# Attention scores as four 64x64 tiles instead of one zero-padded 128x128 matmul, in a fused Linformer and MLP-mixer kernel

## The chip, the cores and the metric

The kernel runs on one core of one Trainium2 chip. The metric is the device time of one execution in microseconds (us): 417.4, 418.6 and 418.67 us in three runs of the kernel before, median 418.6 us. What this measurement can tell from no change is about 0.3%, or 1.3 us.

## What is computed

A Linformer attention on `q`, `k`, `v` of shape (8, 8, 1024, 64), batch, heads, tokens, head width, feeds an MLP mixer; all inputs and the output are float32, the kernel works in bfloat16 with float32 sums.

```python
k_proj = einsum('ks,bhsd->bhkd', E, k)      # 1024 tokens to 64
v_proj = einsum('ks,bhsd->bhkd', F, v)
scores = q @ k_proj.T / 8                   # (1024 x 64) @ (64 x 64) a head
attn   = softmax(scores)                    # over the 64 projected tokens
x      = attn @ v_proj                      # heads side by side: (8, 1024, 512)
u      = x + (relu(x.T @ w_tok1) @ w_tok2).T        # 1024 -> 256 -> 1024 over tokens
out    = u + relu(u @ w_ch1) @ w_ch2                # 512 -> 1536 -> 512 over channels
```

## The kernel before

**The work of a batch.** Eight batches go through a front and a back. The front is: projection of keys and values (`kv_proj`), turning of keys and queries (`k_transpose` and `q_transpose_pe` on TensorE for batches 0 and 1, `k_transpose_dma` and `turn_q` by DMA transposes later), `scores`, `attend`, and the token mixing (`token1...`, `token2...`). Its result `u` is turned, by TensorE for batch 0 and by a DMA transpose (`turn_u`, tile uT) for the others. The back is the channel mixing in two blocks of 512 tokens a batch: `up_set` (line 1193), three sets a block, and `down_block` (line 1301). Up, down and, from batch 2 on, the token products take seven products where the plain scheme takes eight; VectorE makes the sums that this needs.

**Two tokens on the partitions.** Token 8p + si of a batch lies on partition p. A turned query tile qT of a head has the 64 widths of an even si on partitions 0 to 63 and those of the odd si on 64 to 127, and 512 columns. So that one matmul serves both, the turned keys kT hold the same 64x64 block twice on the diagonal of a 128x128 tile, with zeros in the other two blocks (a memset in line 307 puts them there once). `scores` (line 634) is one 128x128 matmul of 512 columns for a head; ScalarE takes the exponential of its bank into the tile a (line 643). The values vb of a head are laid out the same way, twice on the diagonal, each with a column of ones that gives the sum of the softmax; `attend` multiplies 128 columns of a with them (lines 657 and 693, 130 columns), and VectorE divides (reciprocal in lines 669 and 705, multiply in 674 and 710).

**Projection.** `kv_proj` (line 529) uses TensorE in two halves of 64 columns: the keys' product goes to output partitions 0 to 63 and the values' to 64 to 127, alternately, from 128-row operands. From batch 2 on, ScalarE copies the keys twice into kb (which also has zero blocks, line 308) and the values twice into vb, 64x512 each, and a DMA transpose makes kT from kb, 128 x 1024.

**What sets the order.** Nothing is scheduled at run time. A planner holds one list of jobs; the string ORDER gives the order of all of them, SPOTS the PSUM bank of each tile, FILLS the places in that order where a matmul on zeros is put in (`blank`, line 440), so that TensorE does not go idle in the opening. Each engine gets its instructions in that order and works them off in that order; semaphores hold an instruction back until what it needs is there. Loads go through POOL's queue, with eight in flight; the DMA transposes through SP's. ORDER, SPOTS and FILLS come from a search outside of the kernel.

**The opening.** E and F, then q, k and v of batch 0 in pairs of heads, the token weights (wt1, wt2), the channel weights (wc1, wc2) and batch 1 are loaded one behind the other; LOADS and ORDER say in which order. Batch 0 is worked pair by pair as it arrives.

Of the kernel before, what the change touches and what calls it, by code (L numbers as in the profile page):

```python
# [15 lines left out]
    "0P0Q0R0S000T0201030U0W0X040V0s0+1G0-050u0t1I1H0x1J0y0z1L1O101209241N0v1K1P0w131M26111A1B1Q1D0625071S"  # L16
    "1T172A1g18080A1C0B1E0C1a1415191b2C1R1k2B1h1i1o1c1F1l1j1d1n1m161X1p1Y1q2D1s1U1r2E1Z1t0D1u1e1f1x1V1W1v"
    "0E272H2F0G0H1w29281+2V2I211y1-2a0F1z222b20232G2P2W2Q2M2c2J2f2X2S2g2N2K2Y2Z2d2L2R2h2e2T2O2k2i2l2U2t0I"
    "2m2p2n332u2j2x2q2r2o342-2y0J0K2v3B2s300Y2z35313C0Z2w2+320c3T3P0a3R3l3Q3F3U3D3V3J3K360d370e3W3X3Z3m38"
    "0L0N413G3p3Y3a3q3n3b3o0b3S0g0O3c420M0h3r3L3s3E3d390f3M0i3f433e3A3t3g3H0j3u3I4547465044513v48493w5x4g"  # L20
    "4h523x5y5z4k4i4A4j3y534B4J604D4l3N4o4E5-544K5+4m0o614C4F3h4p554r4L3z4n4s0p574R4q0k584u5A4S0q3-4H0l4t"
    "3j0m62634v563O654O646N666P4w594P6O5C404T6Q3+4x6e6W4Q6f6X6g3i674U6T6B6Y6Z696L5I684I3k6U6V4V6R6J6K6a6A"
    "5J6S6b6F6G5D4G6c6d0r5K5M6C4MAH6D6E6j4y4W6H5BAI6r6I0n5N6s6k6l4N4Y6u6t6m6n6h6i6o6v4Z5L5P705O6p4X6w714c"
    "726x5Q6q736z5R4a5a6y6+6-75745S5E7677787B5bAJ7C797H5T7A5c7I4d5U7D7K7E5i7J7LAK6M7NA97M7Q7FAB7G7O7R7S7P"
    "AL4b7T5V5G4z5F4+AAAOAC5W5Y5X7V5j4eAN7UAM7XAQ7W4-5f7Z7YAP7a7c7g5g7e7d7h5h7f5d7i5lAV5kAh5mAW7jAZAb5e5H"
    "Ai7bAX5n5ZAcAaAe7l7pAfAYAd5p7qAmAj817r7sAg7nAnAkAlAuAT7tAxAo5qAvAw7o7u7m82ApAr7wAy85Az5r5o7vAqAsAtA+"
    "B583B0A-5t7x86BB887y847-BC7z7k89B1B6ASB2B7BDAUARB3B880BE8J87B9BF7+8BBAB4BJ8ABM8KBGBK8LBLBHBI8M8NBP8D"
    "BNBS8OBQBO5uBR8Q8b8P8CBTBVBU8EBXBW8RBYBZ8T8y8S8cBaBb8UBc90Bd8+Be918V94Bf5v8zBgAD8WBj92Bh95Bk9E97Bi9F"
    "93Bn968FBo8-Bl9GBr9I98Bs9A9J9HAFBmBp8HBq8I99AEEn8dBuBw8X9CEp9B9L9M8jBxBvBt9WBy9OErEoEq8Z9PAG9X8g8k8h"
    "BzB+5sEj8YEk4f9DB-9aC48iC19Y8mC08lC29bC59dC79Z9c8G9e8nC68e9K8aC89f8oCB8f9g9NEs9iC99QCC8pCDEl8q8uCA9j"  # L30
    "CG9hCH8r8sC3CJE-8vEzCEF09R9oEx8wCFCLE+CNEyCO9p9kCbEv5wF1F4CK9qCP9wEmF5CQF29SF39mCMCR9xCcCIF69U9TCSCf"
    "F7CUCVCgF8Cd9y9tFBCXFCCT8t9uF9FDCYCWEw9VFGCeCtFH9vFACu9lCZCiCaFOCjDWFPCvCw9zChFECxFIDXCyFFFL9+ClCkCz"
    "FJFMDYFN9-FQ9nFRC+FSCmFKCnCoC-A1FTD0FUFVD9DaA2D1DbFWEuDAD3CpA3FXFYDeFZFaEtDfDZDcDdFd9rD4D5CqDh9sIrDB"
    "DiFeA0FbFfItFcCrA5DkFh8xInFgIsIvD2FiCsIoFjA6DoFnIuFoFkA7D7FlFmDHFrD8DpDlDgFpFvDIFsDjFqFtDmDsA4DnFwDt"
    "DJFyDEFxF+D6DFFzDqG0F-DvDGDCG8G1DrDwFuDKG2G3DyG9G5G4DLG6GBE4DMDuGCDzE5DDDxE8DNIpIqIwE9GAGDGFD+GGGEGH"
    "EBDOECE6GIDPGKD-G7J3EAGJGLEDDSJ4E7I-DQIzJ0J1EEEGGRJ2EFJ5J8GSGNDTGPGMEMJ9J6J7JDEHDUDRE0JAJBJEE1EIENGT"
    "GfEOE2GgGVJCEKA8EUGjGWEVJFGOGkJGERJHEWGQELGhESJNGmGiGUETJOGYGXJIGnI+JKDVGZGpGxJLIxGbEXEJGqJMJPHaGyJJ"
    "GaHcEYMrJSJTGcJQGzGdJRJUE3EZHeG-EbGlJVGeIyJWHbG+H0EPJXH2GoGrHdJYJZGsHfHgHiJaJbHjH3JcEQJdEcEaHhJfHsJh"
    "EdJgJiH5MsHlGtJeEfHmJjHoEgH1H6HtJkJmEhHpJlJnH4EiHkGuJoHnJrHDJsGvJpJqH7JvHqH8JtJwH9HAHBJzJxJuJ+HrMvK0"
    "HwK2HxMxK1JyHEK3K4HzJ-K5MtK6HFHuHIKCK9MyHLK7H+MwHvKDMzI0I1HMKFHyKAHCK8EeHNKGI8HGI9GwHJICHKKJIAKHKEHO"  # L40
    "IBIDKKKIKMHPKLH-HQM+KNHHIFKON7IGI2KBHSN8IEKPN3IIHTNCHRKRN4MuKVIJIHI3HUKTIKN5KWNDIQKZN9ILN1M-KaN6KXHW"
    "IRNAKYNBISIMNEKjNHHXNIKUI4NFNGI6IYHYNJKkIZNKNLNRKcKdI7NOKnIOKoKlKfIVNSNPNQNMIWKmIaKQNNKSHVKgKbI5NTIX"
    "NUKeINLeKqK-L0IbNVKhN2IcNYL3KiITNZNWKrNaL4NbIPL6NXIdNcL7IUNdKpIeIfNeKsNfIgL1KtIjKvNgNlN0NhIhNjKwL2L5"
    "L8IkLHL9LBNmKxNiNkKuKzLfNnIlLCQwNoLiLINqNpNrNsLALDIiKyQzLjLkLgLJK+LELFNtNuNvLlNwLmHZNxLwLGLMLxQ-NzNy"
    "N+O1O2LnN-LNLOL+R1LyO4LpLPO6O5O0O8LhR0O9L-LzQ+LQLoM1LSO7LqO3LRLrLTQvImOBOGOALuODOCOELvQyLsMCM2OHQxOJ"
    "M4LtOKM0LKONLLM3M5OIMDR2LUMGOLOOMHM6OPLWMEMJMFOQOSOMM7LVOFLXMKOTMIOVMLOXORLYOZLaR7MOMMRBLbMPMQMUM8R9"
    "R8MNRCOaRDLcREOWMVRARFOdOnMWOoMSMAObMcMBR4RIOrMZRJOeOcOsOpRKOuRNROOYOqR5RPMdLZOvOgOxRGOyRVRHOUMaP3Oh"
    "RWM9MeRLOfOjRSMbR6OiRTMTMfRMOkP4RaRbOlRUMRMgOmP7RQOtRXRRMhRYP5RZMjMXPiOwRcMYPmP6RdReOzMiRfPjO+PkMkMn"
    "P8RgPLR3RhMlPnPARiPlMoRjPBP9PqPoRkUzPpPDMpRlRnPCO-PMRoRpV1PFRmRqPEPrMmMqPtRrV3PNRsRtPuPsPGPHLdP0V5Ru"
    "RvPTPwRzP1V2PIV4RwPJRxRyP+P2R+PUPxPvS1PVS5R-S2PQS0S3S6U+P-PyPzQGS8SAQ0SKQ2QHQ1S9SBQIPKS4Q3QJSCPRS7SL"  # L50
    "SDQ4Q5SFQKSNPSSESHQ6QLSGQ8PWSPPXQNQ7SISOPYSRV0V6U-QASSSMQBQ9QOSTSQPOQCPaSUPPSWSXQMVBPbSVQQVCV7QRV9QY"
    "SJQDSdQPPZPcV8SZVAQZVDVEVFSbQSQTSeSfPeVIShSYSgPfQaSiQgVJVGVKQUSkQWPgQEVNScQhSrVOVPVHPdQdVLVVQeSsSlSv"
    "VWVSSwVMSaQiQfSnStSjSoVQTnVTTmVUSyVXT7VRSuSzToQjSmSxVaVYQXVZQVVcVdVeS-S+QFSpSqVbQkVfQbT0TqT8T1QlQcQn"
    "TBT2T9VgVhQmViTrTCTsVjTEQoTpVkVlQpTAVnQrVpTFTHQsTDTtVqVmTIU2QtVoTuTGT3VrVsVtTwVuTvTJU3TxVvVzVwT5TKU6"
    "TyVxVyU4T+V-TzTPV+U7T6W0U0TLT-U5W1W5U9W6UKT4TNW2UAW3ULU1W7WATQW8QqUCTRW4TMW9TOUOUDUPTUWCU8UMTVWDPhQu"
    "WBTXWEWKWFWHTWUBWGTYTaWITZUNURUETbUSUFTSUQWLWNTcWPTTUTTeWOTdUWWRTiUXWJUUWdTfWZWaWSWMUVTjWeWrWfTgWbWT"
    "WUWgWQUcWsWhWiWcUdWvWkUGTkWVUYUeWtWuWlUkX7UaUIUHUlUhWjWWUmWnUiThUJWXUjX8WwWmXBWyX9UZWoWzUnXAWYWpWqUo"
    "UbW-XCX0UpUfWxW+XEXDXFXGUgUrXHXJXqUqUsXmX1XoXKY6XnUvUtXIX2XPXrY7XuX3UuYAUwXsX5XLX4XNUxX6XpXvXQY8YBYD"
    "XwXxXtXRYEXXXUXyY9XzYGYOXYY0XVTlYHY1XWXMYPYSYQYCXaY2YTYFYRYVXZXbYWY3XcXOYUYXYIXSXeYaXfYJYKYbYgY4XTYM"
    "YYXgYZYcXdYhYeX+YLYiXiYNX-UyXhYlXjYmYdYfYoXkYxYnYjYkYsYpYqYrXlYuYvY5Z5YtYyYwZ7YzY-Y+Z0Z1Z6Z2Z8Z3Z9Z4"  # L60
    "ZA"
)
SPOTS = (
    "3142613427007634307612314207426673103142670116377263077463615421302542313140341042376756766765577757"
    "5677567656575676776765677012402414535120342241300556757665577667657656757670616706243123414252534103"
    "1030217767656565656566664736746140534132101500435323042776765656566656666572764742531530452410441031"
    "0201575666656765656667373675631354342042453105031532566576565656665666657476371031410300534153443125"
    "327676656565666566662726706421140051545432102101214756"
)
FILLS = (9, 9, 14, 14, 14, 14, 14, 14, 16, 16, 16, 16, 16, 16, 27, 27, 27, 42, 42, 72, 81, 81, 84)  # L70
# [118 lines left out]
def kernel(  # L189
# [86 lines left out]
    vb = tile_of([P, H, 2, D1], BF16, "vb")  # L276
    kT = tile_of([P, H, 2, KP], BF16, "kT")
# [4 lines left out]
    kb = tile_of([P, H, 2, D], BF16, "kb")  # L282
# [9 lines left out]
    a_t = [tile_of([P, 2, S2], BF16, f"a{i}") for i in range(2)]  # L292
# [4 lines left out]
    rdn_t = [tile_of([P, 2, 4], F32, f"rdn{i}") for i in range(2)]  # L297
# [9 lines left out]
    nc.vector.memset(kT, 0.0)  # L307
    nc.vector.memset(kb, 0.0)
# [198 lines left out]
    def kv_proj(b, h0, hn, due, block=False, apart=False):  # L507
# [3 lines left out]
        t = 8 * max(cols, 128) / 2400 + 0.22  # L511
        if block:
            k_to = [kb[i * KP : (i + 1) * KP, hs, i, :] for i in range(2)]
        else:
            k_to = [kp[:, hs, i, :] for i in range(2)]
        v_to = [vb[i * KP : (i + 1) * KP, hs, i, 0:D] for i in range(2)]
        of = {"k": (0, k_to, "kb" if block else "kp", ET_sb, k_sb), "v": (KP, v_to, "vb", FT_sb, v_sb)}

        def side(names):
            bk = Bank(stream[0], full=False)  # L520
# [5 lines left out]
            def mm():  # L526
                for si in range(NSI):
                    for n in names:
                        nc.tensor.matmul(  # L529
                            view(n), of[n][3][:, si, :], of[n][4][:, hs, si, :],  # L530
                            start=(si == 0), stop=(si == NSI - 1),
                        )

            pl.add(
                "PE", t, t, mm, reads=[("EFT", 0), ("EFT", 1)] + [(n, h) for n in names for h in heads],
                takes=[bk], prio=due,
                after=[("vb", i, h) for i in range(2) for h in heads] if "v" in names else (),
            ).mms = NSI * len(names)
            unit = scalar() if block else next(sides)
            for n in names:  # L540
# [67 lines left out]
    def q_transpose_pe(hp, due):  # L608
# [19 lines left out]
        )  # L628

    def scores(h, due):  # L630
        bk = Bank(stream[0], full=False)
        pe(
            1, 512,
            lambda: nc.tensor.matmul(  # L634
# [938 lines left out]
```

## Time and profile before

| | |
|---|---|
| median of three runs | 418.6 us (417.4 to 418.67) |
| span of the profiled execution, first to last instruction | 415.5 us |
| granted TensorE clock, mean | 1.000 |
| busy: PE, DVE, ACT, POOL | 409.8, 358.8, 227.4, 66.7 us |
| matmuls | 3845 |
| scores, line 634 | 64 matmuls of 512 columns, 379 ns each |
| projections, line 529 | 192 matmuls of 64 array columns |
| DMA transposes: uT, qT, kT | 14, 12 and 6; 4.3, 5.2 and 3.2 us from issue to landing |
| DMA | 62.47 MB, mean 150 GB/s; 201 to 207 GB/s from 10 to 80 us |

The profile gives the profiled execution no other time than its span; the median of the runs is 3.1 us above it, which is what lies around the span. The duration of one matmul in the table is from its start to its modelled end, and matmuls overlap: what one costs the engine is the distance from its start to the next start, which the timeline shows. So a busy share of PE near 100% does not say by itself that TensorE is at its limit; the distances do.

### The profile page before, as it was taken

Reading aid. Unit: us, or ns where it says so; the run is one execution under the profiler, and the core shown is the slowest. Engines: PE = TensorE matmul, PEld = TensorE weight load, DVE = VectorE, ACT = ScalarE, POOL = GpSimd, SP = SyncE. Lnnn points to the kernel's source line nnn. Section 1 sums busy time; section 2 is a strip of 40 time slices with the busy share of each in tenths; the row PEclk is TensorE's granted clock in tenths of the full one; section 3 lists DMA queues with packets and bytes.
Section 4 is the critical chain, followed back from the end, with each engine's and each line's share of the span. In section 5 each row is a group of like instructions: output and inputs, shape, how many; then the busy total and the mean of one; then the engine's idle time right before and its main releaser. Section 6 shows DMA issues by size and latency. Waiting matters only on the chain.

```text
span 415.5 us, 9448 instructions
## 1 busy us (share of the span) xinstructions
PE 409.8 (99%) x3845; PEld 349.0 (84%) x3845; DVE 358.8 (86%) x774; ACT 227.4 (55%) x434; POOL 66.7 (16%) x105
## 2 busy tenths in 40 slices
PE   8999999999999999999999999999999999999996
PEld 4589888688898889888898888988898889998885
DVE  2489898899899988989988997888999998897696
ACT  1758875376745655564465537365573656254620
POOL 8444111013010400130101220102200010000100
PEclk9999999999999999999999999999999999999999
DMA  8999999996999898679979899488982403212314
GB/s 162 204 202 205 206 206 224 168 138 101 232 167 209 137 233 134 104 170 221 217 106 189 113 184 198 83 165 135 231 152 53 100 11 144 50 53 52 153 50 154
DMA packets 96827, 62.47 MB, mean 150 GB/s; under 512 B 62096, under 2 KB 92304, under 8 KB 96784
## 3 DMA queue, kind: packets, MB, share of 16 engines
q0 software_dynamic: 35088, 45.09, 55.4%
q1 hardware_dynamic: 61056, 16.00, 22.8%
q10 hardware_dynamic: 640, 0.79, 0.5%
q8 instruction: 30, 0.49, 0.5%
q14 instruction: 13, 0.11, 0.1%
HBM read 59.24 MB, written 16.78 MB: 183 GB/s over the span
## 4 chain that ended last, share of the span: by engine, by line
PE 94%; DMA 2%; POOL 2%; DVE 1%; issue 0%; POOLq 0%; DVEq 0%
PE psum L1193 35%; PE psum L1301 35%; PE psum L1004 4%; PE psum L888 4%; PE psum L529 3%; PE psum L634 3%; DMA v_sb<-in_v_dram 2%; PE psum L693 2%; PE psum L657 1%; PE psum L1105 1%; PE psum L748 1%; PE psum L1073 1%; PE psum L724 1%; DVE x_sb L674 1%; POOL k_sb L362 1%; PE psum L618 0%
## 5 line engine op out<-in xcount | busy, mean ns | idle before, releaser
L1301 PEld LDWEIGHTS <-G 128*128 128x128 bf16 x1344 | 130.2, 98 | 17.2 <-issue 0.2
L1301 PE MATMUL psum<-wc_sb,G 128*128 128x256 bf16 x768 | 104.0, 273 | 0.0
L1193 PEld LDWEIGHTS <-wc_sb 128*128 128x128 bf16 x768 | 73.9, 98 | 10.1 <-issue 0.6
L1215 ACT ACTIVATE G<-psum 128x512 bf16<-128x512 f32 x96 | 57.3, 601 | 40.7 <-PE psum L1193 40.2
L1301 PE MATMUL psum<-wT,G 128*128 128x256 bf16 x576 | 77.8, 273 | 0.0
L1229 DVE TENSOR_TENSOR G<-G 128x512 bf16<-128x512 bf16 (+1 forms) x140 | 69.1, 514 | 0.5
L1193 PEld LDWEIGHTS <-wT 128*128 128x128 bf16 x576 | 55.6, 98 | 7.5 <-issue 0.4
L1193 PE MATMUL psum<-uT,wc_sb 128*128 128x256 bf16 x384 | 56.8, 273 | 0.0
L1193 PE MATMUL psum<-S,wT 128*128 128x256 bf16 x384 | 56.8, 273 | 0.0
L1193 PE MATMUL psum<-S,wc_sb 128*128 128x256 bf16 x384 | 56.5, 273 | 0.0
L643 ACT ACTIVATE a<-psum 128x512 bf16<-128x512 f32 x64 | 37.4, 600 | 26.3 <-PE psum L634 25.9
L1341 DVE TENSOR_TENSOR o<-psum,u 128x512 f32<-128x512 f32 x59 | 40.3, 684 | 4.7 <-PE psum L1301 3.2
L1335 POOL DMA_DIRECT2D out_dram<-o x30 | 16.3, 546 | 159.4 <-DVE o L1341 124.6
L1221 ACT COPY ub<-psum 128x512 f32<-128x512 f32 x48 | 28.1, 589 | 21.9 <-PE psum L1193 18.1
L1174 DVE CUSTOM_DVE_ANT_0 G<-psum,ub 128x512 bf16<-128x512 f32 x48 | 32.8, 683 | 6.9 <-PE psum L1193 6.5
L1236 ACT COPY psum<-psum 128x512 f32<-128x512 f32 x48 | 27.7, 577 | 19.3 <-PE psum L1193 7.7
L1174 DVE CUSTOM_DVE_ANT_0 G<-psum,ua 128x512 bf16<-128x512 f32 x48 | 32.8, 684 | 5.8 <-PE psum L1193 3.0
L1221 ACT COPY ua<-psum 128x512 f32<-128x512 f32 x48 | 28.1, 591 | 17.2 <-PE psum L1193 17.0
L362 POOL DMA_DIRECT2D v_sb<-in_v_dram x18 | 13.4, 745 | 132.7 <-DMA uT<-u 76.7
L1193 PE MATMUL psum<-uT,wT 128*128 128x256 bf16 x192 | 28.7, 273 | 0.0
L710 DVE TENSOR_TENSOR x_sb<-psum,rdn 128x512 bf16<-128x512 f32 x40 | 27.5, 688 | 0.9
L634 PE MATMUL psum<-qT,kT 128*128 128x512 bf16 x64 | 22.8, 379 | 0.1
(109 smaller groups left out, 548.2 us busy)
## 6 DMA issues: line engine op xcount, KB each, us to landing
out_dram<-o POOLq DMA_DIRECT2D x30, 512.0 KB, 4.8
k_sb<-in_k_dram POOLq DMA_DIRECT2D x14, 512.0 KB, 9.3
v_sb<-in_v_dram POOLq DMA_DIRECT2D x14, 512.0 KB, 6.5
q_sb<-in_q_dram POOLq DMA_DIRECT2D x14, 512.0 KB, 12.3
wc_sb<-in_moe_w_ch_dram POOLq DMA_DIRECT2D x6, 256.0 KB, 11.6
wc_sb<-in_moe_w_ch_dram POOLq DMA_DIRECT2D x4, 384.0 KB, 15.1
k_sb<-in_k_dram POOLq DMA_DIRECT2D x4, 256.0 KB, 7.4
q_sb<-in_q_dram POOLq DMA_DIRECT2D x4, 256.0 KB, 8.9
```

The costliest lines, as they stand in the source:

```text
L362: return lambda: nc.gpsimd.dma_start(out=dst, in_=src)
L634: lambda: nc.tensor.matmul(bank(bk), kT[:, h].rearrange("p c k -> p (c k)"), qT[:, h].rearrange("p j s -> p (j s)"), start=True, stop=True,),
L643: lambda: nc.scalar.activation(out=a_t[h // 2 % 2][:, h % 2], in_=bank(bk), func=ACT.Exp, scale=scale),
L710: lambda: nc.vector.tensor_tensor(out=x_sb[:, :, h * D : (h + 1) * D].rearrange("p (n c) d -> p n c d", n=2), in0=view()[:, :, :, 0:D], in ...
L1174: nc.vector._custom_dve(TENSOR_ADD_SAT, out=out, in0=in0, in1=in1, s0=FMAX, s1=0.0)
L1193: nc.tensor.matmul(t[:, c, :], w1_of(n, dd, 2 * m + c), a_of(j, n, dd), start=(n in (1, 7) and c == 0 and dd == 0), stop=(c == 1 and dd == 1),
L1215: lambda: nc.scalar.activation(out=G[:, n, cs], in_=view(src), func=ACT.Relu),
L1221: 512, lambda: nc.scalar.copy(out=dst, in_=view("y")), writes=[(name, s % 2)],
L1229: 512 * len(both), lambda: f(out=G[:, n, c], in0=G[:, a, c], in1=G[:, b, c]), ps=False,
L1236: 512, lambda: nc.scalar.copy(out=view("y"), in_=view("x")), takes=[bk["y"]],
L1301: nc.tensor.matmul(to, G[:, G_OF[n], cc, t * P : (t + 1) * P], w2_of(n, cc), start=(n in opens and (t == 0 or alone) and cc == 0), stop=(c ...
L1341: 512, lambda: nc.vector.tensor_add(out=dst, in0=view(src), in1=u_of(sh, dh)),
```

## The change

1. **Scores in quarters.** `scores` takes pairs of heads. For a pair, four matmuls of a 64x64 tile and 512 columns each replace two of 128x128. Each uses one half of the array's rows (even or odd si) and one half of its columns (first or second head of the pair), in the order (0,0), (1,1), (0,1), (1,0). Each row half has a bank of its own; a bank holds both heads on its partitions. Batch 0 does this for one pair at a time (four blocks of four matmuls); the other batches for two pairs at a time (two blocks of eight, 14 blocks in all), which takes four banks at once. The exponentials stay 64 of 128x512, into four tiles a instead of two.
2. **Keys without zero blocks.** kT and kb have half the size, and their two memsets are gone. The keys are still copied twice (kb: 64x512 each, now with a broadcast), the DMA transpose of the keys moves 128 x 512, and `k_transpose` needs one copy instead of two.
3. **Values by pairs.** The two blocks of vb are now the two heads of a pair, not one head twice: each copy is half as wide (64x256 for a whole batch), and the memset of vb is half as wide. `attend` works on a pair and one parity of si, with as many matmuls and VectorE instructions as before, of the same sizes.
4. **Order, banks and fills are all new**, 24 fills instead of 23, and with them the order of the loads and DMA transposes: the first load is q instead of k, and both halves of wt1 are loaded ahead of the last values of batch 0 (v of heads 6 and 7).

```diff
-    def scores(h, due):
-        bk = Bank(stream[0], full=False)
-        pe(
-            1, 512,
-            lambda: nc.tensor.matmul(
-                bank(bk), kT[:, h].rearrange("p c k -> p (c k)"),
-                qT[:, h].rearrange("p j s -> p (j s)"), start=True, stop=True,
-            ),
...
+    def scores(pairs, due):
+        bks = {(g, half): Bank(stream[0]) for g in pairs for half in range(2)}
+
+        def mm():
+            for g in pairs:
+                for half, i in ((0, 0), (1, 1), (0, 1), (1, 0)):
+                    rows, to = (slice(n * D, (n + 1) * D) for n in (half, i))
+                    nc.tensor.matmul(
+                        bank(bks[g, half])[to], kT[rows, 2 * g + i],
+                        qT[rows, 2 * g + i].rearrange("p j s -> p (j s)"), start=True, stop=True,
+                    )
...
-    vb = tile_of([P, H, 2, D1], BF16, "vb")
-    kT = tile_of([P, H, 2, KP], BF16, "kT")
+    vb = tile_of([P, HP, 2, D1], BF16, "vb")
+    kT = tile_of([P, H, KP], BF16, "kT")
...
-    nc.vector.memset(kT, 0.0)
-    nc.vector.memset(kb, 0.0)
...
-                out=kT.rearrange("p h c k -> p h (c k)"), in_=kb.rearrange("p h r d -> p (h r d)")
+                out=kT.rearrange("p (g i) k -> p g (i k)", i=2), in_=kb.rearrange("p g r d -> p (g r d)")
...
-        unit(0.4, lambda t: scores(0, t))
-        unit(0.4, lambda t: scores(1, t))
-        for h in range(H):
-            if h + 2 < H:
-                unit(0.4, lambda t, h=h: scores(h + 2, t))
...
+        unit(1.0, lambda t: scores((0, 1), t))
+        for g in range(HP):
+            if g == 1:
+                unit(1.0, lambda t: scores((2, 3), t))
             for half in range(2):
+                unit(0.5, lambda t, g=g, half=half: attend(g, half, t, 2 if b >= WHOLE else 1))
```

More of the change, by code (lines that the diff above doesn't have):

```diff
@@ L21 @@
[L21 to L35, printed above, removed]
@@ L291 @@
     G_t = [tile_of([P, 7, C2, 2 * P], BF16, f"G{i}") for i in range(2)]
-    a_t = [tile_of([P, 2, S2], BF16, f"a{i}") for i in range(2)]
+    a_t = [tile_of([P, 2, S2], BF16, f"a{i}") for i in range(HP)]
     wait_t = tile_of([P, 2, 2, DH], F32, "wait")
@@ L510, in kv_proj @@
         cols = hn * D
[L511 to L517, printed above, removed]
+        t = 8 * max(cols, 128) / 2400 + 0.03
+        pairs = slice(h0 // 2, (h0 + hn) // 2)
+        of = {"k": (0, ET_sb, k_sb), "v": (KP, FT_sb, v_sb)}
         def side(names):
-            bk = Bank(stream[0], full=False)
+            bk = Bank(stream[0], full=hn == H)
             def view(n):
@@ L577, in k_transpose @@
             prio=due,
-            after=[("kT", i, h) for i in range(2) for h in heads],
-        )
-        unit = next(sides)
-        for c in range(2):
-            rows = slice(c * D, (c + 1) * D)
-            copy(
-                unit, hn * KP, kT[rows, hs, c, :], lambda rows=rows: view()[rows, 0:hn],
-                writes=[("kT", c, h) for h in heads], uses=[bk],
-            )
+            after=[("kT", h) for h in heads],
+        ).mode = 2
+        copy(
+            next(sides), hn * KP, kT[:, hs], lambda: view()[:, 0:hn],
+            writes=[("kT", h) for h in heads], uses=[bk],
+        )
     turned_u, rest = {}, {}
@@ L628, in q_transpose_pe @@
         )
-    def scores(h, due):
-        bk = Bank(stream[0], full=False)
-        pe(
-            1, 512,
-            lambda: nc.tensor.matmul(
-                bank(bk), kT[:, h].rearrange("p c k -> p (c k)"),
-                qT[:, h].rearrange("p j s -> p (j s)"), start=True, stop=True,
-            ),
-            reads=[("kT", 0, h), ("kT", 1, h), ("qT", h)], takes=[bk], prio=due,
-            after=[("a", h % 4)],
-        )
-        act(
-            512,
-            lambda: nc.scalar.activation(out=a_t[h // 2 % 2][:, h % 2], in_=bank(bk), func=ACT.Exp, scale=scale),
-            writes=[("a", h % 4)], uses=[bk],
-        )
@@ new lines, in scores @@
+    def scores(pairs, due):
[7 more added lines that the diff above has]
+                        qT[rows, 2 * g + i].rearrange("p j s -> p (j s)"), start=True, stop=True,
+                    )
+        heads = [2 * g + i for g in pairs for i in range(2)]
+        j = pl.add(
+            "PE", len(pairs) * MM[512], len(pairs) * MM[512], mm,
+            reads=[(n, h) for n in ("kT", "qT") for h in heads], takes=list(bks.values()), prio=due,
+            after=[("a", g, half) for g in pairs for half in range(2)],
+        )
+        j.mms, j.mode = 4 * len(pairs), 3
+        for (g, half), bk in bks.items():
+            act(
+                512,
+                lambda g=g, half=half, bk=bk: nc.scalar.activation(
+                    out=a_t[g][:, half], in_=bank(bk), func=ACT.Exp, scale=scale
+                ),
+                writes=[("a", g, half)], uses=[bk],
+            )
@@ new lines, in attend, with unit, view, mm @@
+    def attend(g, half, due, span):
+        def unit(jn, due):
+            n = len(jn)
+            bk = Bank(stream[0], full=False, span=n)
+            rdn = rdn_t[g % 2][:, 2 * half + jn[0] : 2 * half + jn[0] + n]
+            def view():
+                t = bank(bk) if n == 2 else bank(bk)[:, None, :]
+                return t[:, :, 0 : 4 * D1].rearrange("p n (c i d) -> p n c i d", c=2, d=D1)
+            def mm():
+                for k, jj in enumerate(jn):
+                    for c in range(2):
+                        at = (2 * half + jj) * P
+                        nc.tensor.matmul(
+                            view()[:, k, c].rearrange("p i d -> p (i d)"), a_t[g][:, c, at : at + P],
+                            vb[:, g].rearrange("k i d -> k (i d)"), start=True, stop=True,
+                        )
+            keys = [("rdn", g % 2, 2 * half + jj) for jj in jn]
+            xs = [("x", 2 * g + i, half) for i in range(2)]
+            pe(
+                2 * n, 130, mm,
+                reads=[("a", g, c) for c in range(2)] + [("vb", 2 * g + i) for i in range(2)],
+                takes=[bk], prio=due, after=xs + keys,
+            )
+            pl.add(
+                "DVE", 0.14, 0.18,
+                lambda: nc.vector.reciprocal(out=rdn, in_=view()[:, :, :, :, D]),
+                writes=keys, uses=[bk],
+            )
+            rows = slice(4 * half + 2 * jn[0], 4 * half + 2 * jn[0] + 2 * n)
+            dve(
+                256 * n,
+                lambda: nc.vector.tensor_tensor(
+                    out=x_sb[:, rows, g * P : (g + 1) * P].rearrange("p (n c) (i d) -> p n c i d", c=2, i=2),
+                    in0=view()[:, :, :, :, 0:D],
+                    in1=rdn[:, :, :, :, None].to_broadcast([P, n, 2, 2, D]),
+                    op=ALU.mult,
+                ),
+                reads=keys, writes=xs, uses=[bk],
+            )
+        if span == 2:
+            unit((0, 1), due)
+        else:
+            unit((0,), due)
+            unit((1,), due)
@@ L1424 @@
         q_transpose_pe(hp, due + 1.5)
-        for h in (2 * hp, 2 * hp + 1):
-            scores(h, due + 2)
-        for h in (2 * hp, 2 * hp + 1):
-            for half in range(2):
-                attend(h, half, due + 3)
+        scores((hp,), due + 2)
+        for half in range(2):
+            attend(hp, half, due + 3, 1)
     for p0, pn in PARTS:
```

198 lines of the change are left out of this document (79 added, 119 removed).

## Prediction

> **What bounds the kernel now.** I read the table of stages first, then the chain that ended last, then PE's timeline around a change of its tiling, then its waits.
>
> The table of stages: its columns are the stage in us, then the busy time of PE, PEld, DVE, ACT and POOL.
>
> ```profile
> 0.00:24.00 24.00, 21.57 (x177) 11.93 (x178) 10.89 (x37) 12.11 (x27) 16.11 (x29) 1.00 1.05 186
> 24.00:110.00 86.00, 85.97 (x874) 72.09 (x875) 77.97 (x206) 56.71 (x111) 18.06 (x25) 1.00 1.11 183
> 110.00:412.00 302.00, 302.00 (x2798) 265.02 (x2792) 269.46 (x531) 158.61 (x298) 32.55 (x51) 1.00 0.69 138
> ```
>
> From 24 us on PE is busy without a break. A matmul's duration overlaps the next one's, so this needs a second look, at distances. The chain in order of time ends with 84 matmuls in one piece:
>
> ```profile
> 403.09 9.18 PE psum L1301 x84
> ```
>
> 9.18 / 84 = 0.109 us for 256 columns at the full clock. I took all distances from start to start of the trace's PE rows from 24 to 412 us and set the same pace against each, by its columns (256 in 0.109, 512 in 0.214): hardly 1 us is left over, apart from what the next fence shows. So after 24 us the time is the sum of PE's work. Nothing else can shorten it, and whatever makes PE wait lengthens it.
>
> PE's timeline where the projections switch the array to two halves of 64 columns and back (start, duration, line):
>
> ```profile
> 150.40 0.38 PE L1301 MATMUL psum<-wT,G 128*128 128x256 bf16 x2
> 150.71 0.40 PE L529 MATMUL psum<-k_sb,EFT_sb 128*64 128x512 bf16 x1
> 150.72 0.40 PE L529 MATMUL psum<-v_sb,EFT_sb 128*64 128x512 bf16 x1
> 150.95 0.38 PE L529 MATMUL psum<-k_sb,EFT_sb 128*64 128x512 bf16 x1
> ...
> 152.25 0.38 PE L529 MATMUL psum<-v_sb,EFT_sb 128*64 128x512 bf16 x1
> 152.56 0.61 PE L888 MATMUL psum<-u,wS 128*128 128x256 bf16 x4
> ```
>
> Three prices stand here. Two column halves run side by side: both start within 0.01 us, and a pair takes 0.214 us (150.95 to 152.25 is six pairs and a start), as one full matmul of 512 columns does. Going in costs 150.71 - (150.40 + 2 x 0.109) = 0.09 us, coming out 152.56 - (152.25 + 0.214) = 0.10 us. And the first pair takes 0.24 us, 0.024 more than the rest, for its weights. The Trainium skill ("TensorEngine Tiling (Array Packing)", Key Properties) says that changing the tiling mode drains TensorE; the trace agrees, with 0.09 to 0.10 us each way. It is the rule that speaks against this change.
>
> Ahead of 24 us PE waits for loads. PE's waits (total, times, longest):
>
> ```profile
> PE psum L529 <- DMA v_sb<-in_v_dram: 1.0, 2, 0.6
> ```
>
> Beside this stand 25 matmuls on zeros (line 440, 5.4 us) that only fill. The loads run back to back at some 205 GB/s until 74 us, one of 256 KB every 1.27 us; the last values of batch 0 land at 21.4 us, wt2 at 26.4 us, the first channel weights at 27.7 and 29.1 us.
>
> **The change part by part.** All sums stand against the profiled execution (span 415.5 us, the median of the runs 3.1 us above it; I carry the difference over unchanged).
>
> *Scores, batches 1 to 7.* Before: 56 matmuls of 512 columns, 56 x 0.214 = 12.0 us, all on PE's path and all in the mode of their neighbours. After: 28 pairs of heads, four quarter matmuls each. If the four run side by side as two halves do above, 28 x 0.214 = 6.0 us: 6.0 us less. The trace of before shows no two matmuls on different rows of the array at once, so this has two ends: 0.214 us for four (line 529's pairs), or two after two, 0.43 us (no gain). I take 0.214, since the two halves of line 529 already read two different moving tensors at once, and since here each row half writes a bank of its own.
>
> *Mode switches.* In the two instruction orders PE changes its mode 36 times before and 70 times after; 27 of the new ones lie in batches 1 to 7 (14 blocks, in and out, one shared with a projection). 27 x 0.095 = 2.6 us more.
>
> *Weights at the head of a block.* Four loads instead of two stand ahead of the first four matmuls. Bounds from rows: 0.024 us a block (the first pair above) up to 3 x 0.109 = 0.33 us (the mean duration of line 529's weight load, three more of them in a row). I take 3 x 0.024 = 0.07 us, nearest to the first: 14 x 0.07 = 1.0 us more; the ends are 0.3 and 4.6 us.
>
> *Batch 0.* 8 x 0.214 = 1.7 us become 4 x 0.28 = 1.1 us, with 0.7 us for 7 switches: no change, and it lies among the fills, where waiting for loads hides it.
>
> *Opening.* One fill more, +0.2 us. wt1 comes earlier by two places of 1.27 us, and v of the last two heads later by as much. The first lets token products of early heads fill PE earlier; the second delays the last heads' attend, their eight reciprocals (0.17 us) and multiplies (0.42 us) on VectorE, and the channel block behind them. In the trace these multiplies end at 27.2 us and the first up product starts at 32.0 us with PE dense between; in the new order fewer token products stand behind that start, so one offsets the other. I take 0, with bounds of 1.2 us (one load) either way.
>
> *Copies, memsets and transposes.* Half-wide value copies save ScalarE 12 x (590 - 372) ns = 2.6 us over the run; two memsets of 0.485 us leave VectorE while the first loads are on their way; each of six key transposes moves half as much. ScalarE is 55% busy, and PE never waits for it after 24 us: cost and gain 0, hidden by PE's own work. If VectorE or SP became late, these would be reserve.
>
> *Waits added.* A block of two pairs needs four free banks at once, where one sufficed, and PE works in order: all matmuls behind it wait too. Then ScalarE has four exponentials in a row, 4 x 0.6 = 2.4 us, ahead of the first attend. Both orders are planned so that other products stand between. The trace of before has no such wait; bounds 0 (as before) to 18 blocks x 0.6 us = 10.8 us (each block one exponential late). I take 0.2 us, near the row of before, in which a planned order of the same kind lost hardly 1 us in 388.
>
> Sum: -6.0 + 2.6 + 1.0 + 0 + 0.2 + 0.2 = -2.0 us; span 413.5, time **416.6 us**, 0.5% less.
>
> **The rivals.**
>
> *A: the opening gets shorter.* wt1 arrives while PE would fill; if the last values are not late for it, up to one load of 1.27 us is gained: 415.4 us. For it: 5.4 us of fills. Against: the last values land 2.5 us later.
>
> *B: a DMA transpose is late.* PE reads uT some time after the last token product that feeds it. Counted in the two orders by PE's pace, 7.8 to 12.1 us of matmuls lie between for the first half of a batch before, 7.5 to 9.9 us after. The path needs VectorE's add (0.69 us), its release, and from issue to landing 4.2 us at least, 4.3 in the median, but 7.7 at most in the trace. At 7.7 it is up to 1.5 us late. New transposes of q now stand ahead of it on SP's queue in some batches. Two late ones cost 2 us: 418.6 us. It decides when the landing takes over about 6.5 us at a slack of 7.5.
>
> *C: weights stay in sight inside a block too.* The weights of the second pair of heads would then load only when the first four matmuls are done: 14 x 0.109 = 1.5 us or more, 418.1 us. The Trainium skill ("TensorE: Matmul & The Clock Gate", Part 3) says that a weight load overlaps running matmuls only where their row groups differ, which would bring this about. Against it: line 529's loads, all on the same 128 rows, are hidden at 0.214 us a pair, so there the trace does not agree.
>
> *D: slower; the row halves take turns.* Each four would need 2 x 0.214 us: PE's time for scores is then unchanged, the switches are on top. 28 x 0.214 = 6.0 us more than forecast: **422.6 us**. From 0.07 us more for each four (2.0 / 28) the gain is gone. Against it: separate banks and separate operands.
>
> **How the numbers follow.** Forecast 416.6 us with a chance of 0.52 (its own range 415.5 to 417.3); A 0.10; B 0.20; C 0.08; D 0.07; 0.03 for others. 0.3%, 1.3 us, is about what a measurement of this kernel can tell from no change. Faster by more than that (under 417.3): 0.50 of the forecast and all of A, 0.60. Slower (over 419.9): D, 0.08 of B (four late transposes or more), 0.03 of the rest: 0.18. Within 0.3%: 0.22. The range for 8 in 10 goes from 414.9 (A with the low end of the weights) to 420.3 us (B with three or four late transposes); it leaves out D.
>
> **What would show it.** In PE's timeline of the changed kernel: four starts of the score line within about 0.1 us and the next four 0.214 us later (else D or C); 0.09 to 0.10 us ahead of and behind each block; a total of the score blocks in batches 1 to 7 near 14 x (0.43 + 0.07 + 0.19) = 9.7 us. PE busy in the stages after 24 us without a break (else B: a wait named after uT, kT or qT, or after the exponentials). The first up product near 32 us (earlier: A). The forecast is wrong if PE waits more than 1 us in all after 24 us, or if the opening moves by more than 1 us.

## The result, and the profile after

The changed kernel takes 419.5 us by the median of six runs (419.1 to 420.9), the kernel before, beside it, 417.6 us (417.4 to 418.7). The ratio is 1.005, with a 95% interval from 1.0032 to 1.0068: slower by half a per cent, where 416.6 us and a gain of 0.5% were forecast. The profiled execution took 419.26 us, its span is 417.4 us (before 415.5; forecast 413.5).

The table of stages of the changed kernel, from 24 us on, with the columns of before:

```profile
24.00:110.00 86.00, 85.65 (x887) 71.19 (x885) 77.17 (x205) 54.59 (x107) 18.87 (x27) 1.00 1.08 184
110.00:412.00 302.00, 299.55 (x2824) 260.39 (x2822) 270.11 (x535) 155.44 (x299) 32.00 (x50) 1.00 0.71 135
```

Look at the second line: PE was busy for 302.00 of 302 us before, now for 299.55. The clock is full in both. So PE waits in the long stage where it never did.

What was changed on purpose works. PE's timeline around a block of scores (start, duration, line):

```profile
175.97 0.82 PE L1295 MATMUL psum<-wc_sb,G 128*128 128x256 bf16 x6
176.72 0.63 PE L643 MATMUL psum<-qT,kT 64*64 64x512 bf16 x8
177.28 0.61 PE L1187 MATMUL psum<-S,wT 128*128 128x256 bf16 x4
```

Six matmuls of 256 columns take 6 x 0.109 = 0.654 us, so 176.72 - 175.97 - 0.654 = 0.096 us go into the switch, and the eight quarters with the switch out of the mode take 177.28 - 176.72 = 0.56 us. Start by start, four begin within 0.01 us and the next four 0.24 us later. 14 blocks at 0.558 + 0.095 are 9.1 us, against 12.0 before.

The time that was gained there is lost in PE's waits (total, times, longest); those of before lay in the opening alone:

```profile
PE psum L1295 <- DVE o L1335: 1.4, 2, 0.9
...
PE psum L521 <- DMA k_sb<-in_k_dram: 0.7, 1, 0.7
...
PE psum L643 <- DVE o L1335: 0.3, 1, 0.3
```

Line 1335 is VectorE's first write into an output buffer `o`. The chain that ended last, in order of time (start, duration), says what VectorE waited for:

```profile
150.74 22.70 issue
174.72 8.33 DMA out_dram<-o
...
200.30 9.18 DMA k_sb<-in_k_dram
...
225.28 7.80 DMA out_dram<-o
```

In this execution two output stores and a key load stand on the path, each for 8 to 9 us. Before, the tail of this chain was one piece of 84 matmuls. Why the transfers are late is in POOL's timeline, which issues loads and stores in one order (in brackets the idle time before, and what ended it):

```profile
173.45 0.55 POOL L1329 DMA_DIRECT2D out_dram<-o  x1 [22.71 <-DVE o L1345]
173.99 0.75 POOL L358 DMA_DIRECT2D v_sb<-in_v_dram  x1
174.72 0.56 POOL L1329 DMA_DIRECT2D out_dram<-o  x1
...
199.76 0.55 POOL L1329 DMA_DIRECT2D out_dram<-o  x1 [6.60 <-DVE o L1345]
200.30 0.75 POOL L358 DMA_DIRECT2D k_sb<-in_k_dram  x1
```

The store at 174.72 is that of o2, and VectorE had written o2 by 171.93 (171.25 + 0.68). It stood behind a store of o0, for which POOL sat idle until 173.45, and behind a load. It landed at 183.05, and VectorE, which uses three o buffers in turn, could not write o2 until then; so a bank stayed full and PE waited 0.68 us. The key load at 200.30 stood behind a store that waited 6.6 us. In the kernel before, the corresponding load came ahead of that wait (POOL again):

```profile
185.87 0.78 POOL L362 DMA_DIRECT2D k_sb<-in_k_dram  x1
...
200.53 1.10 POOL L1335 DMA_DIRECT2D out_dram<-o  x2 [13.13 <-DVE o L1351]
```

The last difference is the end. In the timeline of the changed kernel ACT issues the three stores of o0, 0.5 MB, only after the last matmul's start at 413.22:

```profile
413.33 1.39 ACTq L1329 DMA_DIRECT2D out_dram<-o  x3
```

In the timeline of the kernel before, the three stores of this row began ahead of the last matmul's start at 411.99:

```profile
411.06 1.43 ACTq L1335 DMA_DIRECT2D out_dram<-o  x3
```

**The account.** As in the prediction, I set a pace against each distance between starts of PE's rows (256 columns 0.109, a block of eight quarters 0.558, a switch 0.095 us); what is over is lost. The last two columns are experiments, told below.

| us, by the profiled execution | before | changed | s13_again | s18_tail2 |
|---|---|---|---|---|
| first matmul starts | 1.0 | 1.1 | 1.1 | 1.1 |
| matmuls at their pace, switches included | 397.7 | 394.4 | 394.4 | 394.4 |
| fills | 9.1 | 9.5 | 9.5 | 9.5 |
| lost up to 30 us | 3.5 | 3.9 | 3.6 | 3.5 |
| lost from 30 us on | 0.6 | 4.3 | 1.3 | 2.0 |
| last matmul starts | 412.0 | 413.2 | 410.0 | 410.6 |
| from there to the end | 3.5 | 4.2 | 4.3 | 3.5 |
| span | 415.5 | 417.4 | 414.3 | 414.1 |

The change takes 3.3 us from PE's work and adds 3.6 us of waits after 30 us, 0.9 us in the opening and 0.7 us at the end: +1.9, the difference of the spans (the rows are rounded).

### The profile page after: what moved, and what is told of

Its sections match the earlier page's. It is cut to its first block, busy times and chain, and to the rows that moved or that the text cites. A ratio compares the mean times of both kernels' runs of the same rounds, so it can differ in the third digit from the quotient of the medians.

```text
span 417.4 us, 9579 instructions
## 1 busy us (share of the span) xinstructions
PE 408.2 (98%) x3910; PEld 344.7 (83%) x3910; DVE 356.7 (85%) x771; ACT 221.3 (53%) x429; POOL 66.7 (16%) x105
## 4 chain that ended last, share of the span: by engine, by line
PE 73%; DMA 10%; issue 8%; DVE 4%; POOL 3%; ACT 1%; POOLq 0%; DVEq 0%; ACTq 0%
PE psum L1295 29%; PE psum L1187 27%; DMA out_dram<-o 4%; PE psum L998 3%; PE psum L882 3%; PE psum L521 3%; PE psum L678 3%; DMA q_sb<-in_q_dram 3%; DMA k_sb<-in_k_dram 2%; PE psum L643 2%; DVE x_sb L698 1%; DMA uT<-u 1%; PE psum L1099 1%; POOL v_sb L358 1%; PE psum L742 1%
## 5 line engine op out<-in xcount | busy, mean ns | idle before, releaser
L1295 PE MATMUL psum<-wc_sb,G 128*128 128x256 bf16 x768 | 101.4, 273 | 1.5 <-DVE o L1335 1.4
L1295 PE MATMUL psum<-wT,G 128*128 128x256 bf16 x576 | 75.2, 273 | 0.0
L1223 DVE TENSOR_TENSOR G<-G 128x512 bf16<-128x512 bf16 (+1 forms) x140 | 70.3, 516 | 0.8
L698 DVE TENSOR_TENSOR x_sb<-psum,rdn 128x256 bf16<-128x256 f32 (+1 forms) x88 | 46.2, 541 | 1.7
L658 ACT ACTIVATE a<-psum 128x512 bf16<-128x512 f32 x64 | 34.8, 607 | 10.1 <-PE psum L643 9.8
L678 PE MATMUL psum<-vb,a 128*128 128x130 bf16 x256 | 25.3, 220 | 0.2 <-ACT a L658 0.2
```

The costliest lines, as they stand in the source:

```text
L658: lambda g=g, half=half, bk=bk: nc.scalar.activation(out=a_t[g][:, half], in_=bank(bk), func=ACT.Exp, scale=scale),
L678: nc.tensor.matmul(view()[:, k, c].rearrange("p i d -> p (i d)"), a_t[g][:, c, at : at + P], vb[:, g].rearrange("k i d -> k (i d)"), start ...
L698: lambda: nc.vector.tensor_tensor(out=x_sb[:, rows, g * P : (g + 1) * P].rearrange("p (n c) (i d) -> p n c i d", c=2, i=2), in0=view()[:, ...
L1223: 512 * len(both), lambda: f(out=G[:, n, c], in0=G[:, a, c], in1=G[:, b, c]), ps=False,
L1295: nc.tensor.matmul(to, G[:, G_OF[n], cc, t * P : (t + 1) * P], w2_of(n, cc), start=(n in opens and (t == 0 or alone) and cc == 0), stop=(c ...
```

## The experiments

The theory: the quarters gain what they should, and the new order of transfers loses it, by stores and a load that stand behind others in POOL's order, with only three o buffers to wait in. The rivals: sharing of the transfers, whatever their order; waits that only move on when one is mended; quartered scores that are worth nothing. A ratio is to the kernel before, on the same chip. Edits of ORDER are shown as its jobs.

**One transfer at a time.** s1_store:

```diff
-store o0 (841), load v (1185), store o2 (837)
+store o2 (837), store o0 (841), load v (1185)
```

> The changed kernel with one store moved: that of o2 (ready at 171.93, issued at 174.72) goes ahead of the store of o0 for which POOL waits until 173.45. Theory of POOL's order: it is issued at about 172.2 and lands about 2.5 us earlier, DVE's write of o2 at 183.15 no longer waits, TensorE's 0.68 us at 183 is gone, and the span is 416.7 instead of 417.4. Rival, bandwidth: what moves in those microseconds is bounded by the transfers beside it, the store still lands at about 183, and the wait stays. Rival, given back: the wait goes, another of the same size opens later, and the span stays at 417.4.

POOL, and VectorE's write for which PE waited:

```profile
172.73 0.55 POOL L1329 DMA_DIRECT2D out_dram<-o  x1 [21.49 <-DVE o L1335]
173.96 0.55 POOL L1329 DMA_DIRECT2D out_dram<-o  x1 [0.68 <-DVE o L1345]
```

```profile
182.59 0.68 DVE L1335 TENSOR_TENSOR o<-psum,u 128x512 f32<-128x512 f32 x1
```

The write has no wait in front of it any more, PE loses 0.07 us between 110 and 200 us instead of 0.75, and the span is 416.8 us, as the theory had it (416.7).

s2_kload:

```diff
-store o1 (914), load q (1428), store o2 (918), load k (1183)
+load k (1183), store o1 (914), load q (1428), store o2 (918)
```

> The changed kernel with one load moved: the key load issued at 200.30 behind a store that waited 6.6 us goes ahead of the store issued at 191.87. Theory of POOL's order: it is issued at about 189 and lands near 199, the 16 projections at 208.5 start without a wait, TensorE's 0.82 us there is gone, and the span is 416.6 instead of 417.4. Rival, bandwidth: the transfers beside it (the query load, two stores) land later by as much as the key lands earlier, and a wait of 0.5 us or more opens on one of them.

The load is issued at 189.15 and PE's wait at the projections is gone (none over 0.06 us between 200 and 230 us). But the span is 417.1, not 416.6: 0.53 us were lost at 172, ahead of the edit, on a transpose of uT, which landed later in this execution. Nor is the edit shown to be what removed the wait: in s14_after, s6_turns and s7_split, told below, the key load stands where the change had put it, and PE does not wait for it at 208 either.

s3_klate:

```diff
-store o0 (1091), load k (1437), load q (1681)
+store o0 (1091), load q (1681), load k (1437)
```

> The changed kernel with one load moved back: the key load issued at 225.82, half a microsecond behind the store of o0 (7.8 us to landing), goes behind the query load at 234.99. Theory of sharing: the store has the transfers to itself but for the transpose of uT, lands in 4 to 6 us, and TensorE's 1.06 us at 232.75 and 0.30 us at 235 go: span 416.0 to 416.4. Rival: the transpose is what slows the store; it still lands at about 233 and the span stays at 417.4.

PE still lost 1.06 and 0.30 us there. The transfers while the store of o0 was under way, 224.3 to 232.3 us (queue, packets, MB; then KB and us to landing):

```profile
DMA packets 2224, 1.05 MB, mean 131 GB/s; under 512 B 2096, under 2 KB 2096, under 8 KB 2224
...
q1 hardware_dynamic: 2080, 0.52, 47.3%
q0 software_dynamic: 144, 0.52, 28.6%
...
out_dram<-o POOLq DMA_DIRECT2D x1, 512.0 KB, 7.8
uT<-u SPq DMA_TRANSPOSE x1, 8.4
```

The rival of this run was right: the transpose (q1) shares with the store, not the key load, and both move half a megabyte in 8 us. The span of 416.4 us is no gain of the edit: PE lost 0.5 us less up to 24 us in this execution, and 0.7 us less at 208. The Trainium skill ("Trainium Kernel Development and Optimization", Key Constraints) says that transfers issued by SP, ACT and POOL run on the same 16 DMA engines and interleave; the trace agrees, since a store of the same size with less beside it landed in 3.2 us (s5_all, at 319).

s5_all, all three and the last store on SP's queue:

```diff
-            queue = (nc.sync if sh else nc.scalar) if last else nc.gpsimd
+            queue = (nc.sync if sh or t == 1 else nc.scalar) if last else nc.gpsimd
```

> The three moves together, and at the end the last 128 KB store (o0, second half) on SP's queue instead of third on ACT's. Theory (the time was lost to stores and loads in POOL's queue, not to the quartered scores): about 2.9 us of waits and 0.4 us of the end go, 416.2 us by the median, 0.3% below the kernel before and 0.8% below the changed one. Rival (the quartered blocks cost what they save, and the waits only show where it is spent): the waits move on, 419 to 419.5.

417.86 us, ratio 1.0004 (0.9994 to 1.0013): as fast as the kernel before, not 0.3% faster. It lies between the two expectations, and 1.5 us below the changed kernel on the same chip (s14_after, below). The waits at 183 and 208 are gone; the one at 232 (1.04 + 0.30) stays, as in s3_klate, and the end still takes 4.3 us from the last matmul's start (4.2 in the changed kernel).

**Are the quarters worth it?** s6_turns gives each tile its two matmuls in succession:

```diff
-            for g in pairs:
-                for half, i in ((0, 0), (1, 1), (0, 1), (1, 0)):
+            for half, i in ((0, 0), (1, 1), (0, 1), (1, 0)):
+                for g in pairs:
```

> The changed kernel with the eight matmuls of a scores block in another order: each of the four tiles twice in succession (first pair of heads, then second) instead of four different tiles and the four again. If the saving is four tiles at work at once, and TensorE starts matmuls in order, a block then takes 0.95 to 1.1 us to the next start instead of 0.56, and the 14 blocks with two pairs and the 4 of batch 0 (unchanged, one pair each) give 5.5 to 7.5 us more: 425 to 427 us, with other waits taking back up to 2 us of it. Rival (the blocks hide behind other waits and their length costs nothing): within 1 us of the changed kernel's 419.5.

419.3 us, ratio 1.0039 (1.0025 to 1.0053): no change. The time is the rival's, but its reason is not, as PE's timeline says:

```profile
177.13 0.64 PE L643 MATMUL psum<-qT,kT 64*64 64x512 bf16 x8
177.69 0.61 PE L1187 MATMUL psum<-S,wT 128*128 128x256 bf16 x4
```

The block takes 0.56 us as before. The second matmul of a tile does not hold up the first of the next tile. The Trainium skill ("TensorEngine Tiling (Array Packing)", Key Properties) has the tiles operate independently; here that holds against the order of the instructions too. So this run tells nothing of the blocks' worth. s10_rows does, with two 128x64 tiles at once:

```diff
-                        bank(bks[g, half])[to], kT[rows, 2 * g + i],
-                        qT[rows, 2 * g + i].rearrange("p j s -> p (j s)"), start=True, stop=True,
+                        bank(bks[g, half])[to], kT[:, 2 * g + i],
+                        qT[:, 2 * g + i].rearrange("p j s -> p (j s)"), start=True, stop=True,
```

> The changed kernel with its scores in two 128x64 tiles at once instead of four 64x64: each matmul runs over all 128 rows, with keys that have no zero blocks, so that it adds up the two halves of the sequence and the scores are other numbers; only its time counts. If four tiles at once are what saves, a block takes 0.85 to 0.87 us instead of 0.56 and a block of one pair 0.43 instead of 0.34, 4.5 to 5 us in all, 423 to 424.5 us. Rival (the waits cover the scores): under 421.

```profile
184.95 1.05 PE L643 MATMUL psum<-qT,kT 128*64 128x512 bf16 x8
185.94 0.61 PE L1187 MATMUL psum<-uT,wc_sb 128*128 128x256 bf16 x4
```

423.65 us, ratio 1.0140 (1.0123 to 1.0158). A block takes 0.99 us, more than the 0.86 expected, which had left out the switch. The 18 blocks grow by some 6.7 us together, the span by only 4.4. The opening takes up 0.8 us, the growth of batch 0: the first up product starts at 33.60 us in both. From there to the last matmul the 14 blocks grow by 5.9 us and the time by 4.5 (379.62 to 384.09), so PE waits some 1.4 us less: a slower PE meets the same transfers later. This suggests that a part of the quarters' gain was paid out as waits. If so, the same edit must cost more where those waits are mended.

Not all of the waits come from the pace, though. With 0.99 us and a switch, a block is slower here than its four matmuls before (0.86 us), and PE still loses 0.36, 0.39, 0.71 and 0.41 us at 186, 211, 235 to 238 and 328, where the changed kernel has its waits. That part belongs to the new order itself.

**The store that shares.** s7_split stores o0 of that block in halves, the first as soon as it is written:

```diff
+        if j == 6:
+            store(0, (0,))
-        store(0)
+        store(0, (1,) if j == 6 else (0, 1))
```

> The changed kernel with one store in two halves: the 512 KB store of o0 issued at 225.28 (7.8 us to landing beside a transpose of uT) is now a 256 KB store issued as its half is ready, at about 219, and another at 225.3. Theory (too few output buffers for a store that shares the transfers): the second half lands by about 230, DVE's write of o0 at 233.18 and TensorE's 1.06 and 0.30 us go, span 416.0 to 416.4 against 417.4, if the opening is as long. Rival: the transpose takes all of the transfers until 231 to 233, and 0.5 us or more of the wait stays.

POOL's two halves, and VectorE's write of o0:

```profile
217.88 0.72 POOL L1329 DMA_DIRECT2D out_dram<-o  x1
224.09 0.73 POOL L1329 DMA_DIRECT2D out_dram<-o  x1 [5.50 <-DVE o L1335]
```

```profile
230.49 0.68 DVE L1335 TENSOR_TENSOR o<-psum,u 128x512 f32<-128x512 f32 x1
```

No wait in front of the write; PE loses 0.24 us between 200 and 300 us instead of 2.4. The span is 414.8 us: 416.0 to 416.4 were expected of this alone, and in this execution the key load's wait at 208 was absent as well.

s8_best has s1_store, s2_kload, s7_split, the last store on SP, and one swap on VectorE:

```diff
-write o0 (1602), write o1 (1668)
+write o1 (1668), write o0 (1602)
```

> All mends together: the store and the key load moved ahead, the store of o0 in two halves, the last store on SP's queue, and two writes of DVE swapped at 324 (the one whose bank the scores wait for goes first). Of 3.6 us of waits after 30 us some 3 go, and 0.4 us at the end: 416.2 to 416.8 by the median, 0.2 to 0.4% below the kernel before. Rival (the waits move on to the next transfer): 417.5 or more, no faster than the kernel before.

416.61 us, ratio 0.9979 (0.9965 to 0.9992). The kernel ran twice more, beside others:

> The kernel with all mends once more, on the chip of the other runs of this call: 0.1 to 0.35% below the kernel before.

416.48 us, ratio 0.9977 (0.9967 to 0.9986).

> The kernel with all mends, beside it on the same chip: 0.1 to 0.35% below the kernel before, 4.1 to 4.4 us from the last matmul's start to the end.

416.55 us, ratio 0.9974 (0.9961 to 0.9987), and 4.3 us from the last matmul's start to the end. The changed kernel on the chip of s13_again:

> The changed kernel as it is, on the chip of the other runs of this call: 0.3 to 0.7% above the kernel before and 2.5 to 3.2 us above the one with all mends.

419.34 us, ratio 1.0052 (1.0039 to 1.0065): 2.9 us above the mended one. In s13_again PE has none of the three groups of waits shown above; it loses 1.3 us from 30 us on, where the changed kernel lost 4.3. Only the places of a store and a load, one split store, a queue and a swap differ, and the queue was worth nothing (s5_all): so what stood at these places is shown to be the cause of 2.9 us. How it divides is less sure. The waits for the two stores stand in both profiles of the changed kernel (0.68 and 0.82 us at 183, 1.06 + 0.30 at 232 to 235); that for the key load stands in the first alone, and s14_after has another in its place, for a transpose of uT at 127, 0.56 us by the distances (PE's waits):

```profile
PE psum L1187 <- DMA uT<-u: 0.4, 1, 0.4
```

s12_rows is the edit of s10_rows on the mended kernel:

> The kernel with all mends, and its scores in two 128x64 tiles at once, over all 128 rows (other numbers; only its time counts). In the order as it was, the same edit lengthened TensorE's work by 7.3 us and the time by 4.3 us, since the waits shrank by 2.4 us. If the four tiles' gain was given back as waits on transfers in POOL's order, the mended kernel has no such waits to shrink and the edit costs 6 to 7.3 us over the mended kernel run beside it. Rival (the 2.4 us have nothing to do with the mended waits): 4 to 5 us again.

422.22 us, ratio 1.0122 (1.0109 to 1.0135), 5.7 us above s13_again by the medians, 6.6 by the spans. In the order as it was the same edit cost 4.3 us by the medians (423.65 against the 419.3 of s6_turns on its chip). By the timelines, from the first up product to the last matmul, it costs 6.25 us here (376.68 to 382.93) and 4.47 there. So 1.4 to 1.8 us of the quarters' gain had gone into waits. This is shown roughly: the intervals of the ratios leave each cost uncertain by some 0.8 us. By the medians the cost is a little under the 6 to 7.3 us expected. Two waits are new here, the first of them in the opening, at 19 us:

```profile
PE psum L521 <- DMA k_sb<-in_k_dram: 0.8, 1, 0.8
PE psum L643 <- DMA kT<-kb: 0.6, 1, 0.6
```

**The opening.** s11_open, on the mended kernel:

```diff
-attend (114) ... project v of heads 6 and 7 (129)
+project v of heads 6 and 7 (129), attend (114)
```

> The kernel with all mends, and in the opening the eight projections of the last two heads' values (started at 25.0, their load there since about 23.4) ahead of the attend that TensorE waits 0.36 us for at 24.0 (its scores' exponentials come late on ScalarE). If that wait is idle time the projections can fill, 0.3 to 0.4 us go from TensorE's losses between 24 and 30 us and from the span (414.7 to about 414.4), too little for the times to tell. Rival: the values are not there yet, or the attend's x comes later by as much as is filled, and the losses between 24 and 30 us stay at 0.7 us.

417.08 us, ratio 0.9996 (0.9987 to 1.0005), 0.6 us above s13_again: it got worse. The rival's reason holds, the values are not there yet, but the losses between 24 and 30 us grow by 0.6 us where it had them stay. PE's waits:

```profile
PE psum L521 <- DMA v_sb<-in_v_dram: 0.4, 1, 0.4
```

s16_open loads these values earlier as well:

```diff
-load wt1 (13), load v of heads 6 and 7 (11)
+load v of heads 6 and 7 (11), load wt1 (13)
```

> The kernel with all mends, and in the opening the load of the last two heads' values ahead of the second load of the token weights (a place and 1.3 us earlier, 21.9 instead of 23.2), and its projections in TensorE's 0.36 us wait at 24.0. Theory (the losses at 24 to 30 us come from these values being late): losses between 24 and 30 us of 0.3 us instead of 0.7. Rival: the token weights, now 1.3 us later, are waited for at 22 to 23, and the losses up to 30 us stay at 3.6 us or more in all.

Again the rival: the token weights are now what PE waits for, and the span is 416.5 us, with 0.76 us lost at 173 on a late transpose of uT in this execution (PE's waits):

```profile
PE psum L1067 <- DMA wt_sb<-in_moe_w_tok_dram: 1.1, 1, 1.1
```

**The end.** s15_tail, on the mended kernel, moves a product of TensorE:

```diff
-product 4 of o1 t=1 (2195), product 2 of o0 (2179, 2180)
+product 2 of o0 (2179, 2180), product 4 of o1 t=1 (2195)
```

> The kernel with all mends, and in the last microseconds TensorE's product for the first half of o0 (a 256 KB store) ahead of one of the two products for o1's last half, so that 262 KB are stored after the last matmul instead of 524 KB. Theory (the end is bounded by the stores that are left when TensorE stops): from the last matmul's start to the end of the span 3.5 to 3.8 us instead of 4.3, as in the kernel before (3.5), so 0.5 to 0.8 us less: 415.7 to 416.0 where the mended kernel has 416.5. Rival (TensorE waits for ScalarE's last G where the product was moved): the last matmul starts 0.3 us or more later and the time stays.

416.58 us, ratio 0.9988 (0.9967 to 1.0009). Both were right: the time is as in s13_again, the end takes 3.5 us, and PE waits 0.20 + 0.26 us in front of the moved product. s17_both adds s16_open:

> Both of the last two edits on the kernel with all mends: the sum of what the two give, 0.5 to 1.2 us below 416.5 if both theories hold, no change if both rivals do.

417.88 us, ratio 1.0011 (1.0001 to 1.0022): the loss of s16_open again. In s15_tail ScalarE's two last writes of G had changed places; s18_tail2 puts them back:

```diff
-write G (2124), write G (2142)
+write G (2142), write G (2124)
```

> The last kernel but two (the product for o0's first half moved ahead at the end) with ScalarE's two last writes of G in the order in which TensorE finishes their sums; in s15_tail they stood the other way round, and TensorE waited 0.46 us for the second. Theory: the wait goes, the end stays at 3.5 us after the last matmul's start, and the time is 0.5 to 0.8 us below the mended kernel run beside it. Rival: ScalarE is late by its own 1.1 us for the two, a wait of 0.2 us or more stays, and the gain is under 0.4 us.

415.96 us, ratio 0.9958 (0.9943 to 0.9973), the fastest kernel here, 0.6 us below s19_best beside it. The stores of o0 now start at 409.69, 0.9 us before the last matmul, instead of after it:

```profile
409.69 1.39 ACTq L1329 DMA_DIRECT2D out_dram<-o  x2
410.07 1.64 SPq L1329 DMA_DIRECT2D out_dram<-o  x2
```

The gain is the theory's, though a wait of 0.25 us for ScalarE stays, as the rival had it. So the 0.7 us at the end are the order of the last products, not the queue of the last store.

## Why the prediction was wrong

- **What bounds the kernel:** right, with its consequence, that whatever makes PE wait lengthens the time.
- **Scores, switches, weights:** -6.0 + 2.6 + 1.0 = -2.4 us were forecast, 9.1 - 12.0 = -2.9 measured. Four at once and 0.095 us a switch hold; the weights at the head of a block cost 0.03 us instead of 0.07. Batch 0 and the rest of PE's work gave 0.4 us more. C and D fall by the timeline.
- **Waits added: the step that failed.** This term of the sum was mis-sized: 0.2 us was taken, from the row of before "in which a planned order of the same kind lost hardly 1 us". Measured: 3.6 us more from 30 us on. That is inside its bounds of 0 to 10.8 us, but these were made of banks and exponentials, and the slack was counted for uT alone. The waits came from stores of o and, in some executions, from a key load or a transpose of uT. For stores and loads the text had no term, although the new order of POOL was at hand; 2.9 us of the time went when those were mended.
- **B, a late transfer:** right in kind. Its price of 2 us was short of the 3.6 measured, the transfers that cost most were others, and it came on top of the opening and the end. Late uT transposes came too, in some executions: 0.53 us at 172 in s2_kload, 0.56 at 127 in s14_after. That 419.5 us lies inside the range for 8 in 10 is luck: its upper part was made of late transposes of uT alone.
- **Opening:** 0.2 us forecast, 0.9 measured: 0.4 of fills, 0.15 of a later first matmul, 0.3 of waits up to 30 us. "One offsets the other" was not so, but it is within the bounds of 1.2 us given; A fell. It stays open what would shorten it: two attempts moved the wait to another load.
- **The end:** not in the sum at all, and 0.7 us. The prediction had set aside what follows PE's last matmul, but the order of the last products decides how many stores are left then.
- **From the span to the time:** the 3.1 us carried over are a median of three times less the span of one execution, a shorter one. Each run on record that has both shows 1.7 to 2.4 us, in the median 1.8; by that a span of 413.5 is 415.3 us. So the forecast was further off than its time says: the span came out 3.9 us longer than forecast, 3.4 of it waits after 30 us, 0.7 each the opening and the end, less 0.9 that PE's work gained beyond the forecast.

Its own test, "wrong if PE waits more than 1 us in all after 24 us", was the right one.

## What to carry to other kernels

When a matrix engine that bounds a kernel gets faster, transfers that are fed or freed by its pace can lose slack, and a new order can take slack from them at any pace: count the slack of every store and load in the new order, not only of the transfer that looks tight. In an in-order queue that issues loads and stores, look for each entry at what waits in front of it: a store whose data comes late holds up a finished store, and a load that others need. A gain that shows in the timeline and not in the time is found by slowing the part down again, before and after the mend: what it then costs more is what the waits had swallowed. And a wait that one profile shows is looked for in a second profile of the same kernel before a mend is credited with it.

## What the runs showed of the hardware

- Eight 64x64 matmuls of 512 columns take 0.56 us to the next start in either order, also when the second matmul of a tile stands directly behind its first (after, s6_turns). As eight matmuls in two 128x64 tiles they take 0.99 us (s10_rows). Both hold the switch out of the mode.
- A transpose of uT and a 512 KB store that run together take 8.4 and 7.8 us at 131 GB/s (s3_klate); a store of that size took 3.2 us with less beside it (s5_all), so when a store is issued says little of when it lands.
- The opening of one and the same order differs between executions: PE's losses up to 24 us were 3.2 and 2.9 us in two profiles of the changed kernel, and 0.3 us of a span say nothing in single runs.
